# The first four units of a linear-attention and MLP kernel: another order of bonus products, loads, masks and transposes

## The chip, the cores and the metric

The kernel runs on one core of a Trainium2 chip. The metric is the device time of one execution in microseconds (us); several runs are given by their median.

## The reference

The first half is a recurrent attention (RWKV) over batch 4, 8 heads, 768 steps and head size 48. For every head it keeps a 48 x 48 state:

```python
for t in range(S):
    cur = np.einsum('bhd,bhe->bhde', u[None] * kt, vt)
    y[:, :, t] = np.einsum('bhd,bhde->bhe', rt, state + cur)
    state = w[None, :, :, None] * state + np.einsum('bhd,bhe->bhde', kt, vt)
```

The term with u is the bonus of the current step: for each step and head it is the sum over d of r times u times k, times v. The second half takes y as a matrix x of 3072 rows (batch by step) and 384 columns through an MLP: `h = x @ w_in` (384 x 2048), `g = h * sigmoid(h)`, `out = g @ w_out` (2048 x 384).

## The kernel before

The 768 steps are cut into six chunks of 128. A unit is one chunk of one batch entry; unit i is batch i mod 4 of chunk i div 4, so there are 24 units, and units 0 to 3 are the first chunk of the four batch entries. Within a chunk the recurrence is turned into matrix products with decayed r and k.

For unit i the steps have short names, which the order below uses:

- `lr`, `lk`, `lv` (line 71): the loads of r, k and v, 192 KB each, issued on SP's queue. Units 0 to 3 are loaded ahead of the order (lines 103 to 115); k of unit 0 is issued by ScalarE (ACT). Eight buffers of each are there.
- `T` (turn, line 251): 16 transposes on TensorE, eight for r and then eight for k. `rT`, `kT` (line 257): VectorE (DVE) multiplies them with the powers of the decay.
- `A01`, `A23` (line 284): the products of k and r for two units together, 64 small matmuls. `am` (line 291): DVE masks the product, with maskM for even units and maskX for odd ones.
- `ku`, `ru` (lines 211 and 215): the bonus on GpSimd (POOL), k times u and then r times that. `rd` (line 224): DVE sums over d. `vu` (line 229): POOL multiplies v by the sum.
- `v16` (line 238): ACT casts v; for an odd unit two more copies (`vx`, lines 241 and 242) swap its halves.
- `Y` (line 306): masked product times v. `y16` (line 334): DVE adds `vu`. `yT` (line 372): three transposes on TensorE, and `xT` (line 376): ACT copies them to x.
- `kc` (line 219): POOL decays k. `S` (line 318): the state product, and `st` (lines 348 and 349): DVE copies it out.
- `L` and `G` (lines 387 and 395): a block of the first MLP product, with the two units that it covers, and its activation on ACT. `L0.0` and `L0.2` are the first blocks for units 0 and 1, and `L0.4`, `L0.6` need the second quarter of w_in. The second MLP product is at lines 408 and 433.
- `i_q` (line 84) and `i_o` (line 89): loads of a quarter of w_in or w_out, 384 KB, issued by POOL.
- `pads`: ACT fills the unused columns of r and k buffers 4 to 7, eight small copies (line 155). `lnw`, `eK`, `lamK`, `lnwb`, `lamC`, `wb`, `mx`: the powers of the decay, and maskX.
- A prefix `n*` puts n matmuls of 128 x 512 on a tile of zeros (`spin`, line 161) before the step; they compute nothing that is used.

There is no scheduler: the kernel is written under a manual schedule, and an order written out by hand (line 485) is walked from left to right. Each step puts its instructions at the end of its engine's queue, and each engine takes its own in that order, waiting where an operand or a buffer is not ready. So the place of a word in the text counts only against other words of the same engine. Short-lived tiles rotate through buffers (two for most); products, transposed y and MLP blocks share four PSUM buffers.

After this order a loop (line 518) takes the later units in pairs, with pieces of the MLP of the chunk before as filling work for TensorE. The loop calls `bonus_products` (line 205), so the change of the bonus reaches it as well.

Of the kernel before, what the change touches and what calls it, by code (L numbers as in the profile page):

```python
# [8 lines left out]
FP = mybir.dt.float32  # L9
F16 = mybir.dt.float16  # L10
AF = mybir.ActivationFunctionType
ALU = mybir.AluOpType
# [3 lines left out]
def kernel(  # L16
# [11 lines left out]
    nc = tc.nc  # L28

    B, H, S, D = r.shape  # L30
# [10 lines left out]
    NIN = 8  # L41
# [4 lines left out]
    wrk = ctx.enter_context(tc.tile_pool(name="wrk", bufs=2))  # L46
# [3 lines left out]
    def unit(i):  # L50
        return divmod(i, B)
# [9 lines left out]
    u_bc = cst.tile([128, H, D], FP)  # L61
    rin = [big.tile([128, H, 64], FP, name=f"rin{i}") for i in range(NIN)]
    kin = [big.tile([128, H, 64], FP, name=f"kin{i}") for i in range(NIN)]
    vin = [big.tile([128, H, D], FP, name=f"vin{i}") for i in range(NIN)]
    kc = [big.tile([128, H, 64], F16, name=f"kc{i}") for i in range(NIN)]
    st = [big.tile([PR, NP, PW], FP, name=f"st{b}") for b in range(B)]
# [4 lines left out]
    def ld(i, dst, src, eng=nc.sync):  # L71
        sc, b = unit(i)
        eng.dma_start(
            out=dst[i % NIN][:, :, 0:D],
            in_=src[b, :, sc * C:sc * C + C, :].rearrange("h t d -> t h d"))

    def load(i):
        if i >= NU:
            return
        for dst, src in ((rin, r), (kin, k), (vin, v)):  # L80
            ld(i, dst, src)
# [29 lines left out]
                                            ap=[[0, 128], [D, H], [1, D]]))  # L111
    ld(0, vin, v)
    ld(1, vin, v)
    load(2)
    load(3)
    nc.vector.memset(ones, 1.0)
    for i in range(B):
        nc.vector.memset(rin[i][:, :, D:64], 0.0)
# [1 line left out]
    for b in range(B):  # L120
# [13 lines left out]
        out=maskM, in_=maskM, compare_op=ALU.is_ge, fill=0.0,  # L134
# [10 lines left out]
    eK = cst.tile([PR, NP, C], FP)  # L145
    lamR = cst.tile([PR, NP, C], FP)
    lamK = cst.tile([PR, NP, C], FP)
    lnw_bc = cst.tile([128, HD], FP)
    lamC = cst.tile([128, H, D], FP)
# [52 lines left out]
    def L(i):  # L202
        return live.setdefault(i, {})

    def bonus_products(i):
        bonus_ku(i)
        bonus_rku(i)

    def bonus_ku(i):
        L(i)["ku"] = wrk.tile([128, H, D], FP, name="ku")  # L210
        nc.gpsimd.tensor_tensor(out=L(i)["ku"], in0=kin[i % NIN][:, :, 0:D], in1=u_bc, op=ALU.mult)  # L211

    def bonus_rku(i):
        L(i)["rku_f"] = wrk.tile([128, H, D], FP, name="rku_f")
        nc.gpsimd.tensor_tensor(out=L(i)["rku_f"], in0=rin[i % NIN][:, :, 0:D], in1=L(i)["ku"],  # L215
                                op=ALU.mult)

    def decayed_k(i):
        nc.gpsimd.tensor_tensor(out=kc[i % NIN][:, :, 0:D], in0=kin[i % NIN][:, :, 0:D],  # L219
# [246 lines left out]
    def piece(word, f):  # L466
# [11 lines left out]
        "am": masked, "v16": cast_v, "kc": decayed_k,  # L478
        "vu": bonus_v,
        "Y": outputs_y, "S": outputs_s, "y16": evict_y, "yT": turn_y, "xT": copy_x,  # L480
        "st": state, "stb": state16, "ku": bonus_ku, "ru": bonus_rku, "rd": bonus_sum,
        "r16": cast_r, "sd": decayed_state, "i_q": ld_win, "i_o": ld_wout,
        "lr": lambda i: ld(i, rin, r), "lk": lambda i: ld(i, kin, k), "lv": lambda i: ld(i, vin, v),
    }
    order = """
        lnw eK lamK mx clear lr4 lk4 lv4 lr5 lk5 lv5 lr6 lk6 lv6 lr7 lk7 lv7 4*T0 ku0 rT0 kT0
        1*T1 rT1 kT1 v160 ru0 rd0 ku1 v161 3*A01 wb ru1 am0 rd1 vu0 lnwb i_q0 lamC pads am1 vu1
        4*Y0 y160 T2 kT2 2*Y1 y161 ku2 ru2 rT2 yT0 xT0 i_q1 yT1 xT1 v162 T3 kT3 rT3 ku3 ru3 rd2
        v163 4*A23 vu2 i_q2 rd3 vu3 am2 am3 L0.0 G0.0 L0.2 G0.2 Y2 y162 Y3 y163 kc0 yT2 xT2 L0.4
        G0.4 kc1 yT3 xT3 L0.6 G0.6 S0 st0 kc2 T4 kT4 rT4 kc3 L2.0 G2.0 S1 L2.2 G2.2 st1 ku4 v164  # L490
        L2.4 G2.4 S2 L2.6 G2.6 st2 ru4 i_q3 r164 L4.8 G4.8 S3 L4.9 G4.9 st3 rd4 ku5 L4.10 G4.10
        T5 kT5 rT5 L4.11 G4.11 vu4 ru5 i_o0 A45 rd5 am4 r165 v165 L4.12 G4.12 vu5 kc4 L4.13
        G4.13 am5 sd4 kc5 Y4 S4 y164 st4 L4.14 G4.14 sd5 i_o1 Y5 S5 y165 st5 L4.15 G4.15 yT4 xT4
        yT5 xT5 T6 kT6 rT6 ku6 ru6 i_o2 H0 H1 v166 r166 H2 H3 T7 kT7 rT7 ku7 i_o3 v167 r167 H4
        ru7 rd6 stb4 stb5
    """
    for word in order.split():
        if "*" in word:
# [19 lines left out]
    for i in range(B + 2, NU, 2):  # L518
# [3 lines left out]
        if i > B + 2:  # L522
            for n in nxt:
                bonus_products(n)
                decayed_k(n)
        if i > B + 2:
            masked(i)
            masked(i + 1)
        else:
            bonus_v(i)  # L530
            decayed_k(i)
            decayed_state(i)
            masked(i)
            bonus_sum(i + 1)
            masked(i + 1)
            bonus_v(i + 1)
            decayed_k(i + 1)
            decayed_state(i + 1)
            for n in nxt:
                bonus_products(n)  # L540
                decayed_k(n)
# [60 lines left out]
```

## Time and profile before

Durations are in us. "Window" is a stretch of the profiled execution.

| what | value |
| --- | --- |
| median of 13 runs | 195.35 (194.24 to 196.98) |
| the profiled execution: run, and span from first to last instruction | 194.70, 193.0 |
| mean granted TensorE clock of the span | 0.991 |
| one bonus product on POOL, L211 or L215 | 1.00 |
| one `vu` (L229), one `kc` (L219) on POOL | 0.83, 1.00 |
| one sum (L224), one mask (L291), one `y16` (L334), one `rT` or `kT` (L257) on DVE | 0.54, 1.22, 0.56, 0.68 |
| one cast of v (L238), one half of `vx` (L241, L242), one `xT` (L376) on ACT | 0.51, 0.51, 0.48 |
| issue of a quarter of w_in by POOL (L84) | 0.80 to 0.93 |
| a load of r, k or v from issue to landing, median | 4.1 to 4.2 |
| a quarter of w_in from issue to landing, median | 6.8 |
| DMA engines' busy share, 20 to 25 us (overlapping packets count twice) | 1.24 |

One bonus product waited: `ku` of unit 0 for u, 3.2 us. In the first 50 us ACT waited 8.6 us for MLP products, and DVE 3.9 us each for transposes (L251) and for bonus products (L215). From 50 us to 150 us the windows show TensorE busy all the time.

The page gives busy time by engine, then 40 slices of the span with a digit for each engine, then the chain of work that ended last. The timeline gives single instructions with start and length and, in brackets, the idle time before them and what ended it.

### The profile page before, as it was taken

The page shows a single profiled execution, that of the slowest core. Times are in us where ns is not written, and L with a number is a line of the kernel's source. Part 1 is how long each engine was busy: PE and PEld are TensorE (multiplying, and loading weights), DVE is VectorE, ACT ScalarE, POOL GpSimd, SP SyncE. Part 2 cuts the span into 40 slices and gives each one's busy share as a digit, 9 for nine tenths or more (in the row PEclk, how much of TensorE's full clock was granted, in tenths as well). Part 3 has the DMA queues.
Part 4 walks back from the last instruction along what each step waited for, and adds up shares of the span by engine and source line. Part 5 has one row for each costly group of instructions (what it writes and reads, how often), then busy time and mean ns, then how long its engine had stood idle before and what let it go on. Part 6 is the DMA issues. An engine that isn't in the chain of part 4 may idle for free.

```text
span 193.0 us, 5626 instructions
## 1 busy us (share of the span) xinstructions
PE 184.4 (96%) x2306; PEld 118.5 (61%) x2306; DVE 102.7 (53%) x188; ACT 108.3 (56%) x212; POOL 120.2 (62%) x159
## 2 busy tenths in 40 slices
PE   7988899989999999999999999999999999999994
PEld 2644684667766886655556665566655656644563
DVE  6577769764782682672672673673574364200120
ACT  5398277759371493176792276791376781089300
POOL 8399994999999939929829839839837430000000
PEclk9996999999999999999999999999999999999999
DMA  5999979999948568249259278177287101320022
GB/s 103 209 182 158 231 146 179 167 202 220 158 107 176 176 117 193 63 104 199 71 107 200 66 163 187 25 140 170 61 183 168 40 5 44 82 82 0 3 82 82
DMA packets 90267, 24.35 MB, mean 126 GB/s; under 512 B 83329, under 2 KB 90242, under 8 KB 90242
## 3 DMA queue, kind: packets, MB, share of 16 engines
q1 hardware_dynamic: 85136, 20.59, 49.3%
q0 software_dynamic: 3712, 3.15, 10.9%
q10 hardware_dynamic: 1394, 0.26, 0.7%
q8 instruction: 18, 0.29, 0.6%
q14 instruction: 7, 0.06, 0.1%
HBM read 20.65 MB, written 4.72 MB: 131 GB/s over the span
## 4 chain that ended last, share of the span: by engine, by line
PE 76%; POOL 13%; issue 3%; DMA 3%; ACT 2%; SPq 1%; DVE 1%; POOLq 0%
PE ops L408 31%; PE hps L387 27%; PE att L284 7%; PE att L251 4%; POOL ku L211 3%; POOL kc L219 3%; DMA u_bc<-in_u_dram 3%; POOL vu L229 2%; POOL rku_f L215 2%; PE yp L306 2%; PE yp L301 2%; POOL win L84 2%; PE sp L318 1%; PE ops L433 1%; ACT gT L395 1%
## 5 line engine op out<-in xcount | busy, mean ns | idle before, releaser
L387 PE MATMUL hps<-xT,win 128*128 128x512 f16 (+1 forms) x360 | 68.2, 337 | 0.7 <-ACT xT L376 0.5
L395 ACT ACTIVATE gT<-hps 128x512 f16<-128x512 f32 x96 | 56.2, 598 | 21.1 <-PE hps L387 18.9
L408 PE MATMUL ops<-wout,gT 128*128 128x384 f16 x368 | 64.0, 326 | 0.0
L408 PEld LDWEIGHTS <-gT 128*128 128x128 f16 x368 | 34.7, 98 | 22.2
L387 PEld LDWEIGHTS <-win 128*128 128x128 f16 x360 | 33.3, 98 | 24.2 <-issue 1.1
L229 POOL TENSOR_TENSOR vu<-vin,rku 128x384 f32<-128x384 f32 x24 | 19.8, 830 | 27.1 <-DVE rku L224 27.1
L414 ACT COPY osb<-ops 128x384 f32<-128x384 f32 x20 | 9.6, 478 | 43.4 <-PE ops L408 43.4
L291 DVE TENSOR_TENSOR am<-att,maskM 128x1024 f16<-128x1024 f32 x12 | 14.7, 1223 | 32.3 <-PE att L284 32.3
L211 POOL TENSOR_TENSOR ku<-kin,u_bc 128x384 f32<-128x384 f32 x24 | 24.1, 1003 | 4.8 <-DMA u_bc<-in_u_dram 3.2
L215 POOL TENSOR_TENSOR rku_f<-rin,ku 128x384 f32<-128x384 f32 x24 | 24.1, 1002 | 1.7
L219 POOL TENSOR_TENSOR kc<-kin,lamC 128x384 f16<-128x384 f32 x24 | 23.8, 999 | 0.0
L284 PEld LDWEIGHTS att<-rT,kT 48*64 48x64 f32 x768 | 18.0, 135 | 6.7 <-issue 3.5
L284 PE MATMUL att<-rT,kT 48*64 48x128 f32 (+1 forms) x768 | 20.4, 250 | 1.2 <-DVE rT L257 0.8
L257 DVE TENSOR_TENSOR rT<-att,lamR 112x512 f32<-112x512 f32 x24 | 16.4, 684 | 9.3 <-ACT gT L395 4.0
L334 DVE TENSOR_TENSOR y<-yp,vu 128x384 f16<-128x384 f32 x24 | 13.3, 556 | 13.6 <-issue 4.8
L257 DVE TENSOR_TENSOR kT<-att,lamK 112x512 f32<-112x512 f32 x24 | 16.4, 682 | 4.0 <-PE att L251 3.9
L291 DVE TENSOR_TENSOR am<-att,maskX 128x1024 f16<-128x1024 f32 x12 | 14.6, 1214 | 0.0
L224 DVE TENSOR_REDUCE rku<-rku_f 128x8 f32<-128x384 f32 x24 | 12.4, 544 | 3.9 <-POOL rku_f L215 3.9
L329 POOL TENSOR_TENSOR sdec<-st,wCT 112x384 f32<-112x384 f32 x16 | 13.2, 825 | 0.0
L238 ACT CAST v<-vin 128x384 f16<-128x384 f32 x24 | 11.4, 511 | 3.3 <-DMA vin<-in_v_dram 3.3
L272 ACT CAST rT<-rT 112x512 f16<-112x512 f32 x20 | 12.4, 619 | 0.3 <-DVE rT L257 0.2
L306 PEld LDWEIGHTS <-am 128*128 128x128 f16 x192 | 9.7, 97 | 4.3 <-DVE am L291 2.8
(64 smaller groups left out, 161.8 us busy)
## 6 DMA issues: line engine op xcount, KB each, us to landing
rin<-in_r_dram SPq DMA_DIRECT2D x24, 192.0 KB, 4.1
vin<-in_v_dram SPq DMA_DIRECT2D x24, 192.0 KB, 4.2
kin<-in_k_dram SPq DMA_DIRECT2D x23, 192.0 KB, 4.2
out_dram<-osb SPq DMA_DIRECT2D x23, 192.0 KB, 2.2
win<-in_moe_w_in_dram POOLq DMA_DIRECT2D x4, 384.0 KB, 6.8
wout<-in_moe_w_out_dram POOLq DMA_DIRECT2D x4, 384.0 KB, 6.4
xT<-y SPq DMA_TRANSPOSE x18, 2.3
kin<-in_k_dram ACTq DMA_DIRECT2D x1, 192.0 KB, 3.5
```

The lines of the kernel that those rows point to most:

```text
L211: nc.gpsimd.tensor_tensor(out=L(i)["ku"], in0=kin[i % NIN][:, :, 0:D], in1=u_bc, op=ALU.mult)
L215: nc.gpsimd.tensor_tensor(out=L(i)["rku_f"], in0=rin[i % NIN][:, :, 0:D], in1=L(i)["ku"], op=ALU.mult)
L219: nc.gpsimd.tensor_tensor(out=kc[i % NIN][:, :, 0:D], in0=kin[i % NIN][:, :, 0:D], in1=lamC, op=ALU.mult)
L229: nc.gpsimd.tensor_tensor(out=L(i)["vu"], in0=vin[i % NIN], in1=L(i)["rku"].unsqueeze(2).broadcast_to([128, H, D]), op=ALU.mult)
L257: nc.vector.tensor_tensor(out=L(i)[key].rearrange("p g (y t) -> p y g t", y=2), in0=L(i)["t"][0:PR, :, x], in1=lam.rearrange("p g (y t) -> ...
L284: nc.tensor.matmul(a[e][o0:o0 + HC, j, p, c0:C], kT[r0:r0 + D, p, s0:s0 + HC], rT[r0:r0 + D, p, c0:C], start=True, stop=True)
L291: nc.vector.tensor_tensor(out=am.rearrange("p h g c -> p (h g) c"), in0=L(i)["a"].rearrange("p h g c -> p (h g) c"), in1=(maskX if crossed ...
L306: nc.tensor.matmul(L(i)["y"][:, h, :], L(i)["am"][:, j, p, :], L(i)["vy"][:, h, :], start=not sc, stop=(not sc or j == 1))
L334: nc.vector.tensor_tensor(out=L(i)["y16"], in0=L(i)["y"], in1=L(i)["vu"], op=ALU.add)
L387: nc.tensor.matmul(hps[:, f, :], win[:, q, (ft + f) * 128:(ft + f + 1) * 128], xts[sc][:, q, b0:b0 + nb, :].rearrange("p b t -> p (b t)"), ...
L395: nc.scalar.activation(out=gts[sc][:, ft:ft + m, b0 * C:(b0 + nb) * C], in_=hpss[b0, ft], func=AF.Silu)
L408: nc.tensor.matmul(opss[b], gts[sc][:, ft, b * C:(b + 1) * C], wout[:, ft, :], start=(ft == 0), stop=(ft == NFT - 1))
```

## The change

- The bonus is r times k first (`rk`) and the result times u afterwards (`ru`), in all 24 units; before it was k times u and then r times that.
- r and k of units 2 and 3 are issued before v of units 2 and 3. The loads themselves are the same.
- In the order: `rk1` comes before `ru0`; on POOL `vu1` comes before the first weight load, `vu3` and `kc0` before the third; `am0` stands before `ru1` in the text. The transposes `T3` with `kT3` and `rT3` come before `yT1` on TensorE and before `y161` on DVE, and `rT2` comes before `y161`. `yT1` comes behind `A23`, and `xT1` behind the casts of v of units 2 and 3 and behind `pads` on ACT. The eighteen matmuls on zeros are spread otherwise.
- From `yT2` on the order is as before, with `rk` for `ku`.

```diff
-    load(2)
-    load(3)
+    for dst, src in ((rin, r), (kin, k)):
+        ld(2, dst, src)
+    for dst, src in ((rin, r), (kin, k)):
+        ld(3, dst, src)
+    ld(2, vin, v)
+    ld(3, vin, v)
...
     def bonus_products(i):
-        bonus_ku(i)
+        bonus_rk(i)
         bonus_rku(i)
...
-        L(i)["ku"] = wrk.tile([128, H, D], FP, name="ku")
-        nc.gpsimd.tensor_tensor(out=L(i)["ku"], in0=kin[i % NIN][:, :, 0:D], in1=u_bc, op=ALU.mult)
+        L(i)["rk"] = wrk.tile([128, H, D], FP, name="rk")
+        nc.gpsimd.tensor_tensor(out=L(i)["rk"], in0=kin[i % NIN][:, :, 0:D],
+                                in1=rin[i % NIN][:, :, 0:D], op=ALU.mult)
...
-        nc.gpsimd.tensor_tensor(out=L(i)["rku_f"], in0=rin[i % NIN][:, :, 0:D], in1=L(i)["ku"],
-                                op=ALU.mult)
+        nc.gpsimd.tensor_tensor(out=L(i)["rku_f"], in0=L(i)["rk"], in1=u_bc, op=ALU.mult)
...
-        lnw eK lamK mx clear lr4 lk4 lv4 lr5 lk5 lv5 lr6 lk6 lv6 lr7 lk7 lv7 4*T0 ku0 rT0 kT0
-        1*T1 rT1 kT1 v160 ru0 rd0 ku1 v161 3*A01 wb ru1 am0 rd1 vu0 lnwb i_q0 lamC pads am1 vu1
-        4*Y0 y160 T2 kT2 2*Y1 y161 ku2 ru2 rT2 yT0 xT0 i_q1 yT1 xT1 v162 T3 kT3 rT3 ku3 ru3 rd2
-        v163 4*A23 vu2 i_q2 rd3 vu3 am2 am3 L0.0 G0.0 L0.2 G0.2 Y2 y162 Y3 y163 kc0 yT2 xT2 L0.4
+        lnw eK lamK mx clear lr4 lk4 lv4 lr5 lk5 lv5 lr6 lk6 lv6 lr7 lk7 lv7 4*T0 rk0 rT0 kT0
+        1*T1 rT1 kT1 rk1 ru0 rd0 v160 v161 3*A01 wb am0 ru1 vu0 rd1 am1 vu1 lnwb lamC i_q0 1*Y0
+        y160 T2 kT2 rT2 2*Y1 rk2 1*yT0 xT0 ru2 3*T3 kT3 rT3 v162 y161 rk3 i_q1 3*A23 v163 pads
+        yT1 xT1 ru3 rd2 vu2 rd3 vu3 am2 am3 L0.0 G0.0 L0.2 G0.2 Y2 y162 Y3 y163 kc0 i_q2 yT2 xT2
...
```

More of the change, by code (lines that the diff above doesn't have):

```diff
@@ L205, in bonus_products, with bonus_rk @@
     def bonus_products(i):
-        bonus_ku(i)
+        bonus_rk(i)
         bonus_rku(i)
-    def bonus_ku(i):
-        L(i)["ku"] = wrk.tile([128, H, D], FP, name="ku")
-        nc.gpsimd.tensor_tensor(out=L(i)["ku"], in0=kin[i % NIN][:, :, 0:D], in1=u_bc, op=ALU.mult)
+    def bonus_rk(i):
+        L(i)["rk"] = wrk.tile([128, H, D], FP, name="rk")
+        nc.gpsimd.tensor_tensor(out=L(i)["rk"], in0=kin[i % NIN][:, :, 0:D],
+                                in1=rin[i % NIN][:, :, 0:D], op=ALU.mult)
     def bonus_rku(i):
         L(i)["rku_f"] = wrk.tile([128, H, D], FP, name="rku_f")
-        nc.gpsimd.tensor_tensor(out=L(i)["rku_f"], in0=rin[i % NIN][:, :, 0:D], in1=L(i)["ku"],
-                                op=ALU.mult)
+        nc.gpsimd.tensor_tensor(out=L(i)["rku_f"], in0=L(i)["rk"], in1=u_bc, op=ALU.mult)
     def decayed_k(i):
@@ L480 @@
         "Y": outputs_y, "S": outputs_s, "y16": evict_y, "yT": turn_y, "xT": copy_x,
-        "st": state, "stb": state16, "ku": bonus_ku, "ru": bonus_rku, "rd": bonus_sum,
+        "st": state, "stb": state16, "rk": bonus_rk, "ru": bonus_rku, "rd": bonus_sum,
         "r16": cast_r, "sd": decayed_state, "i_q": ld_win, "i_o": ld_wout,
@@ L485 @@
     order = """
-        lnw eK lamK mx clear lr4 lk4 lv4 lr5 lk5 lv5 lr6 lk6 lv6 lr7 lk7 lv7 4*T0 ku0 rT0 kT0
-        1*T1 rT1 kT1 v160 ru0 rd0 ku1 v161 3*A01 wb ru1 am0 rd1 vu0 lnwb i_q0 lamC pads am1 vu1
-        4*Y0 y160 T2 kT2 2*Y1 y161 ku2 ru2 rT2 yT0 xT0 i_q1 yT1 xT1 v162 T3 kT3 rT3 ku3 ru3 rd2
-        v163 4*A23 vu2 i_q2 rd3 vu3 am2 am3 L0.0 G0.0 L0.2 G0.2 Y2 y162 Y3 y163 kc0 yT2 xT2 L0.4
[L490 to L495, printed above, removed]
+        lnw eK lamK mx clear lr4 lk4 lv4 lr5 lk5 lv5 lr6 lk6 lv6 lr7 lk7 lv7 4*T0 rk0 rT0 kT0
+        1*T1 rT1 kT1 rk1 ru0 rd0 v160 v161 3*A01 wb am0 ru1 vu0 rd1 am1 vu1 lnwb lamC i_q0 1*Y0
+        y160 T2 kT2 rT2 2*Y1 rk2 1*yT0 xT0 ru2 3*T3 kT3 rT3 v162 y161 rk3 i_q1 3*A23 v163 pads
+        yT1 xT1 ru3 rd2 vu2 rd3 vu3 am2 am3 L0.0 G0.0 L0.2 G0.2 Y2 y162 Y3 y163 kc0 i_q2 yT2 xT2
+        L0.4 G0.4 kc1 yT3 xT3 L0.6 G0.6 S0 st0 kc2 T4 kT4 rT4 kc3 L2.0 G2.0 S1 L2.2 G2.2 st1 rk4
+        v164 L2.4 G2.4 S2 L2.6 G2.6 st2 ru4 i_q3 r164 L4.8 G4.8 S3 L4.9 G4.9 st3 rd4 rk5 L4.10
+        G4.10 T5 kT5 rT5 L4.11 G4.11 vu4 ru5 i_o0 A45 rd5 am4 r165 v165 L4.12 G4.12 vu5 kc4
+        L4.13 G4.13 am5 sd4 kc5 Y4 S4 y164 st4 L4.14 G4.14 sd5 i_o1 Y5 S5 y165 st5 L4.15 G4.15
+        yT4 xT4 yT5 xT5 T6 kT6 rT6 rk6 ru6 i_o2 H0 H1 v166 r166 H2 H3 T7 kT7 rT7 rk7 i_o3 v167
+        r167 H4 ru7 rd6 stb4 stb5
     """
```

## The prediction

> **What bounds the kernel now.** I read the page first, for who is busy and where the clock fell; then the chain of waits in order of time; then the timeline of the first 27 us engine by engine; last the windows. From the page:
>
> ```profile
> PE 184.4 (96%) x2306; PEld 118.5 (61%) x2306; DVE 102.7 (53%) x188; ACT 108.3 (56%) x212; POOL 120.2 (62%) x159
> ...
> PEclk9996999999999999999999999999999999999999
> ...
> PE 76%; POOL 13%; issue 3%; DMA 3%; ACT 2%; SPq 1%; DVE 1%; POOLq 0%
> ```
>
> TensorE is 96% busy, and one slice, the fourth (14.5 to 19.3 us), had a low clock. The chain, from its list of pieces (start, length, what):
>
> ```profile
> 3.31 4.91 DMA u_bc<-in_u_dram
> ...
> 8.37 1.00 POOL ku L211
> ...
> 22.25 3.86 POOL kc L219 x4
> ...
> 46.07 1.55 PE att L284 x56
> ```
>
> From about 46 us to the end the chain is TensorE alone, so a change of the first units is worth only what it moves that point. Before it the chain names POOL from 8.37 us on. That is a list of who was late, not of how much is gained if POOL is early: the instructions from 15 to 26 us decide that (start, length, engine, line; in brackets the idle time before and its releaser):
>
> ```profile
> 15.56 1.09 ACT L376 COPY xT<-yT 128x384 f16<-128x384 f16 x2
> 16.54 0.93 ACT L238 CAST v<-vin 128x384 f16<-128x384 f32 x2
> 18.02 0.51 ACT L242 COPY vx<-v 64x384 f16<-64x384 f16 x1
> 18.90 1.84 PE L284 MATMUL att<-rT,kT 48*64 48x128 f32 x64
> 20.68 1.48 PE L387 MATMUL hps<-xT,win 128*128 128x256 f16 x12
> 20.80 1.22 DVE L291 TENSOR_TENSOR am<-att,maskM 128x1024 f16<-128x1024 f32 x1 [0.30 <-PE att L284]
> 23.21 0.37 PE L306 MATMUL yp<-vx,am 128*128 128x48 f16 x8 [0.76 <-DVE am L291]
> 25.33 0.33 PE L318 MATMUL sp<-v,kc 128*128 128x96 f16 x4
> 25.70 0.35 DVE L348 CAST stb<-sp 48x192 f16<-48x192 f32 x1 [1.46 <-PE sp L318]
> ```
>
> The point that carries the rest is S0 (the state product of unit 0, L318, 25.33). From 25.70 DVE runs without a gap over 0.04 us until 33.98 (st0, kT4, rT4, st1 to st3, rd4, kT5, rT5); rd4 releases POOL's vu4, which waited 2.4 us, and from there vu4, ru5, vu5, kc4, kc5 and S5 follow to 38.9 and the chain to A67 at 46.07. So I take a shift of S0 as the shift of the end.
>
> ```profile
> 12.71:16.12 3.41, 2.27 (x34) 1.19 (x32) 3.41 (x6) 3.30 (x10) 3.31 (x5) 1.00 0.77 129
> 16.12:19.53 3.41, 3.41 (x33) 1.89 (x36) 1.96 (x4) 2.32 (x5) 3.31 (x4) 0.50 1.10 179
> 19.53:22.94 3.41, 2.92 (x80) 2.44 (x72) 2.69 (x3) 1.19 (x2) 3.39 (x5) 1.00 1.26 226
> ```
>
> These windows (columns: length, then PE, PEld, DVE, ACT, POOL busy, then clock, DMA share, GB/s) are cut at the clock's own edges: after 3.41 us with PE busy 2.27 the clock is 0.50 for 3.41 us; after 2.92 it stays 1.00.
>
> **What the Trainium skill says.** "TensorE: Matmul & The Clock Gate", Part 1, says that the array's clock is halved according to recent activity, judged in free-running windows of 3413 ns. The trace agrees in length (16.12 to 19.53), and in effect: warm-up matmuls (L161) start 0.22 us apart at 7 us and 0.42 at 17 us. The page gives no busy share that decides; the trace brackets it between 2.27 and 2.92. The same page, Part 2, says that matmuls stay in program order and only weight loads are pulled ahead: so L0.0 holds up everything behind it. "DMA: Bandwidth & Descriptors", Queues, rings and completion order, says that each DMA engine takes turns between the queues that have work. The trace fits: v3, issued at 12.71, took 4.2 us to land while the first weight load (issued 13.22) streamed.
>
> **The change part by part**, against this execution (span 193.0, run 194.70; the median of 13 runs is 195.35, 0.65 more).
>
> POOL, r by k first. Same count of products, same shapes, 1.00 us each (rows L211, L215). rk0 needs k0 and r0 (1.42 + 3.5 = 4.9), POOL is free at 5.1: 5.1 to 6.1. rk1 waits for k1 (2.52 + 3.9 = 6.4): 6.6 to 7.6. ru0 still waits for u (3.31 + 4.91 = 8.22): 8.37 to 9.37; ru1 to 10.33. Before they ended at 10.45 and 12.49. So 3.25 us of idle POOL take two products, and the sums come 1.1 and 2.2 us sooner.
>
> Masks. On DVE the order rd0, am0, rd1, am1 stays. rd0 9.40; am0 must wait for A01 (8.56 + 1.55 = 10.11): 10.17 to 11.39; rd1 to 11.87; am1 11.8 to 13.0 (before 14.21). vu1 11.95 to 12.79; first weight load 12.73, 0.5 us sooner. Then rk2 waits for k2, which lands as before (8.21 + 4.8 = 13.0): 13.7 to 14.7, ru2 to 15.75, rk3 to 16.7, second weight load 16.65 (before 17.00), ru3 18.47 (before 19.91). POOL's lead ends at 1.4 us. The third weight load goes behind vu3 and kc0: 20.98 for 20.63. It landed at 28.3 and is used at 29.55: costs nothing with 1.2 us to spare. The fourth comes about 1.4 us sooner, but nothing waits for it there.
>
> Loads. SP issues the same loads with r3 and k3 in the places of v2 and r3. v2 landed at 8.98 + 4.6 = 13.6, k3 at 10.48 + 4.5 = 15.0; so r3 comes at 13.6, k3 by 15.0 at most (I take 14.3), v2 at 15.0. v3 stays last, at 12.71 + 4.2 = 16.9. Bound for the new mix: v3 unchanged, or up to 0.5 us later because the weight load starts 0.5 us sooner and shares the engines. I take 16.9 and keep the other for the range.
>
> TensorE. Eighteen warm-up matmuls before and after, spread otherwise. T2 waits for k2 as before (13.05 to 13.48), two warm-ups, Y1 13.87, one, yT0 14.45, three, T3 at 15.35 instead of 16.06 and at full clock: its window from 12.7 has few holes. T3 ends 16.0 (before 17.15), kT3 and rT3 1.29 us of DVE: 17.35. A23 17.4 to 18.95 at the 1.55 us of A01 (before 18.90 to 20.74). Gain 1.8 us, of which 0.7 from T3's place and the rest from the clock.
>
> Behind it yT1, moved from before T3 to after A23: 18.80 to 19.14. Its copy xT1 is where the gain goes. ACT's order is now xT0, v2, v3, two vx, eight pads, xT1. xT0 14.85 to 15.3, v2 to 15.8, v3 waits for its load: 16.96 as before; vx until 18.53; pads 1.69 us (eight, 0.20 apart): until 20.2; xT1 0.48: about 20.6. L0.0 needs xT1: 20.68, the very time of before. TensorE has nothing from 19.14 to 20.68, and am2 and am3, ready at 20.2 and 21.35 instead of 22.02 and 23.15, wait behind L0.0 and L0.2. What is left: Y2 22.08 as before, Y3 at once (22.35 for 23.21), y2 to 23.06 (before 23.62), yT2 23.12, L0.4 not before the second weight load lands (17.00 + 6.7 = 23.7; I take 23.4), S0 = L0.4 + 1.47 = 24.9. Sum at full clock: 24.92 - 25.33 = -0.4.
>
> But the windows now hold that 1.5 us hole. With the edges of this trace, 19.53 to 22.94 has 1.48 (L0.0, L0.2) plus 0.65 (Y2, Y3), 2.1 busy: less than the 2.27 that halved the clock. Elsewhere in phase, windows from 17.6 to 21.0 or 18.6 to 22.0 have 1.9. Then 3.41 us follow at half clock. With the trace's edges: yT2 0.33, L0.4 0.65 doubled to 1.3, yT3 0.3, L0.6 1.3: S0 at 26.35, +1.0 against before. If it falls on L0.0 and L0.2 (1.30 of issue doubled) and the small steps behind: S0 at 25.9, +0.6. The old low clock is already in the 25.33. I take +0.7.
>
> The steady state: rk reads r and k where ku read k; rows and waits are otherwise the same, buffers of r come free one product sooner (SP's waits for POOL's products there, 2.0 and 1.5 us, end no chain). Zero.
>
> **Rivals.** Forecast: hole and low clock, +0.7, 196.0 (own range 195.7 to 196.6), chance 0.52. For it: the 16.9 of v3 and the ACT order, both free of guesses; against: no trace shows whether 1.9 to 2.1 suffices.
> Rival one, not slower: the clock stays up behind the hole. S0 at 24.9, -0.4: 194.95; it decides if the threshold lies under 1.9 (against: 2.27 halved it), or if the clock falls earlier, in the thin stretch 10.9 to 13.4, where only one warm-up is left before Y0 (about 2.7 busy, between the brackets): then T3 and A23 go slower, the hole closes and the sum is 0 to -0.4. Chance 0.28.
> Rival two: v3 later by 0.5 us with the weight load's start, on top of the low clock: L0.0 21.2, sum +1.2, 196.5. Chance 0.12; against: v3's last packets may be its own.
> Rival three: ACT gets to xT1 sooner than I think (v3 at 16, pads quicker); L0.0 then waits for the first weight load, 20.19 - 0.5 = 19.7, Y2 21.1, Y3 21.4, S0 by the second weight load at 24.6 to 24.9, -0.4 to -0.8: 194.7. Chance 0.08.
>
> **How the numbers follow.** About 0.3% (0.59 us) is what a measurement can tell here. The range goes from 194.8 (rival one and half of three) to 196.8 (rival two and the forecast's worst phase). Slower by over 0.59: two thirds of the forecast, all of rival two and a share for what I have not seen, 0.52. Within: 0.36. Faster: rival three and the edge of rival one, 0.12.
>
> **What would show it.** Right: rk0 near 5.1, ru0 at 8.4, A23 starting near 17.4, xT1 behind the pads near 20.1, TensorE idle before L0.0 at 20.7, a window of clock 0.50 starting between 19.6 and 23.0, S0 later than 25.5. Wrong: L0.0 before 20.3; no low clock after 19 us; S0 before 25; or an end that does not move with S0, which would mean slack after 34 us that I have not seen.

## The result and the profile after

| | before | after |
| --- | --- | --- |
| median | 195.28 of 48 runs (194.24 to 198.23) | 198.59 of 11 runs (196.52 to 200.12) |
| profiled execution: run, span | 194.70, 193.0 | 198.53, 196.8 |
| mean granted TensorE clock of the span | 0.991 | 0.983 |

The changed kernel is slower: its time is 1.0151 of that before, with an interval of 1.0116 to 1.0185, and its median is 3.3 us higher. In this section and the next, ratios leave out executions over 1.5% above the fastest of their own kernel (two of twelve here), which changes the reading of two experiments, where all executions are given too. The lines of the changed kernel stand four higher than before's: L391 is the first MLP product, L380 `xT`, L322 the state product, L242 the cast of v, L245 and L246 `vx`, L159 the pads, L215 `rk`, L220 `ru`.

First the page of after: the engines, the clock in 40 slices, the chain by engine, and the costliest group of TensorE (busy time, mean of one in ns, idle time before it and the releaser). The last line is the same group on the page of before.

```profile
PE 184.8 (94%) x2306; PEld 119.2 (61%) x2306; DVE 102.8 (52%) x188; ACT 108.5 (55%) x212; POOL 120.2 (61%) x159
...
PEclk9999769999999999999999999999999999999999
...
PE 74%; SPq 10%; issue 4%; POOL 4%; DMA 3%; ACT 2%; DVE 1%; POOLq 0%
...
L391 PE MATMUL hps<-xT,win 128*128 128x512 f16 (+1 forms) x360 | 70.1, 344 | 4.0 <-ACT xT L380 3.8
```

```profile
L387 PE MATMUL hps<-xT,win 128*128 128x512 f16 (+1 forms) x360 | 68.2, 337 | 0.7 <-ACT xT L376 0.5
```

No engine has noticeably more work. The row that stands out is L391: in front of it TensorE was idle 0.7 us before and 4.0 us now, nearly all of it for `xT`, and it is busy 70.1 us instead of 68.2 for the same 360 products, which goes with the lower clock (slices five and six, where before had one in slice four). The chain has changed its names as well: POOL went from 13% to 4%, and SP's queue has come up to 10%. Its list of pieces, in order of time (start, length, what), shows where:

```profile
19.06 2.61 SPq L73
21.71 6.42 DMA kin<-in_k_dram
29.28 7.24 issue
...
49.88 1.55 PE att L288 x56
```

The part of A67 at which TensorE takes over starts at 49.88 instead of 46.07: the same 3.8 us as the span. Ahead of it the chain now follows SP and the load of a k. Read as a cause, that would say that the loads of later units are late. Experiment one tests this reading against the other one, which the timeline of the same kernel gives:

```profile
5.32 1.00 POOL L215 TENSOR_TENSOR rk<-kin,rin 128x384 f32<-128x384 f32 x1 [0.20 <-DMA kin<-in_k_dram]
8.38 1.95 POOL L220 TENSOR_TENSOR rku_f<-rk,u_bc 128x384 f32<-128x384 f32 x2 [0.57 <-DMA u_bc<-in_u_dram]
...
17.76 1.55 PE L288 MATMUL att<-rT,kT 48*64 48x128 f32 x60 [0.27 <-DVE rT L261]
...
19.13 0.51 ACT L242 CAST v<-vin 128x384 f16<-128x384 f32 x1 [3.07 <-DMA vin<-in_v_dram]
19.25 0.34 PE L376 MATMUL yT<-ident,y 128*128 128x128 f16 x3
20.20 0.51 ACT L246 COPY vx<-v 64x384 f16<-64x384 f16 x1
20.72 0.30 ACT L159 CAST rin<-idle 128x128 f32<-128x128 f16 x1
22.12 0.29 ACT L159 CAST kin<-idle 128x128 f32<-128x128 f16 x1
22.32 0.47 ACT L380 COPY xT<-yT 128x384 f16<-128x384 f16 x1
22.84 2.72 PE L391 MATMUL hps<-xT,win 128*128 128x256 f16 x12 [3.25 <-ACT xT L380]
29.15 0.33 PE L322 MATMUL sp<-v,kc 128*128 128x96 f16 x4
29.52 0.35 DVE L352 CAST stb<-sp 48x192 f16<-48x192 f32 x1 [2.51 <-PE sp L322]
```

POOL's products, the masks and A23 are as early as they were meant to be. Then ACT waits 3.07 us for v of unit 3, which lands at 19.1; the cast, two `vx` and eight pads follow (20.72 to 22.32 for the pads alone), and only then `xT1`. Its transposes were done at 19.6. L0.0 starts at 22.84 where it started at 20.68, and S0 follows at 29.15 for 25.33. From S0 to TensorE's last instruction it is 164.8 us in both profiles, so the end has moved with S0.

The windows of after show the second half of the loss (length, then PE, PEld, DVE, ACT and POOL busy, clock, DMA share, GB/s):

```profile
18.24:21.65 3.41, 1.35 (x55) 1.16 (x48) 3.18 (x4) 2.46 (x8) 3.25 (x5) 1.00 1.25 220
21.65:25.06 3.41, 2.22 (x11) 1.56 (x11) 0.07 (x1) 1.73 (x6) 3.39 (x5) 0.50 1.09 188
25.06:28.48 3.42, 3.02 (x31) 2.38 (x30) 1.02 (x2) 1.14 (x3) 2.77 (x4) 0.50 1.02 193
```

The hole leaves 1.35 us of work in the first window, and the next one is at half clock. That next one still holds a part of the hole and is busy only 2.22 us; after it the clock stays at 0.50 for one window more. A mean of 0.983 over the span is two such windows; nine of twelve executions of after have that mean to within 0.001, two have 0.991 (one window), one has 0.974.

How late v3 was stands in the DMA issues between 13.2 and 13.8 us (size, then us from issue to landing):

```profile
vin<-in_v_dram SPq DMA_DIRECT2D x1, 192.0 KB, 5.9
...
win<-in_moe_w_in_dram POOLq DMA_DIRECT2D x1, 384.0 KB, 5.7
```

Before, v3 was issued at 12.71 and the first weight load at 13.22, and v3 took 4.2 us. Now the weight load is issued at 12.76 and v3 behind it at 13.18: v3 takes 5.9 us. Whether the one makes the other is asked in experiments three, five and ten.

### The profile page after: what moved, and what is told of

Same layout as the page of the kernel before. It is cut to its first block, busy times and chain, and to the rows that moved or that the text cites. A ratio compares the mean times of both kernels' runs of the same rounds, so it can differ in the third digit from the quotient of the medians.

```text
span 196.8 us, 5624 instructions
## 1 busy us (share of the span) xinstructions
PE 184.8 (94%) x2306; PEld 119.2 (61%) x2306; DVE 102.8 (52%) x188; ACT 108.5 (55%) x212; POOL 120.2 (61%) x159
## 4 chain that ended last, share of the span: by engine, by line
PE 74%; SPq 10%; issue 4%; POOL 4%; DMA 3%; ACT 2%; DVE 1%; POOLq 0%
PE ops L412 31%; PE hps L391 26%; SPq L73 9%; PE att L288 7%; PE att L255 4%; DMA kin<-in_k_dram 3%; PE yp L310 2%; PE yp L305 2%; PE sp L322 1%; PE ops L437 1%; ACT gT L399 1%; POOL kc L223 1%; SPq L110 1%; POOL vu L233 1%; POOL rk L215 1%
## 5 line engine op out<-in xcount | busy, mean ns | idle before, releaser
L391 PE MATMUL hps<-xT,win 128*128 128x512 f16 (+1 forms) x360 | 70.1, 344 | 4.0 <-ACT xT L380 3.8
L391 PEld LDWEIGHTS <-win 128*128 128x128 f16 x360 | 34.1, 100 | 28.3 <-issue 4.5
L233 POOL TENSOR_TENSOR vu<-vin,rku 128x384 f32<-128x384 f32 x24 | 19.8, 829 | 32.8 <-DVE rku L228 32.8
L215 POOL TENSOR_TENSOR rk<-kin,rin 128x384 f32<-128x384 f32 x24 | 24.1, 1005 | 2.5 <-DMA kin<-in_k_dram 2.5
L220 POOL TENSOR_TENSOR rku_f<-rk,u_bc 128x384 f32<-128x384 f32 x24 | 23.9, 999 | 2.1 <-DMA u_bc<-in_u_dram 0.6
L242 ACT CAST v<-vin 128x384 f16<-128x384 f32 x24 | 11.5, 511 | 6.4 <-DMA vin<-in_v_dram 6.4
L333 POOL TENSOR_TENSOR sdec<-st,wCT 112x384 f32<-112x384 f32 x16 | 13.2, 825 | 0.0
L420 DVE COPY osb<-ops 128x384 f32<-128x384 f32 x3 | 1.7, 557 | 19.8 <-PE ops L412 19.8
```

What stands on the lines that cost most here:

```text
L215: nc.gpsimd.tensor_tensor(out=L(i)["rk"], in0=kin[i % NIN][:, :, 0:D], in1=rin[i % NIN][:, :, 0:D], op=ALU.mult)
L220: nc.gpsimd.tensor_tensor(out=L(i)["rku_f"], in0=L(i)["rk"], in1=u_bc, op=ALU.mult)
L233: nc.gpsimd.tensor_tensor(out=L(i)["vu"], in0=vin[i % NIN], in1=L(i)["rku"].unsqueeze(2).broadcast_to([128, H, D]), op=ALU.mult)
L391: nc.tensor.matmul(hps[:, f, :], win[:, q, (ft + f) * 128:(ft + f + 1) * 128], xts[sc][:, q, b0:b0 + nb, :].rearrange("p b t -> p (b t)"), ...
```

## The experiments

The theory was that the loss is the hole in front of L0.0 (`xT1` behind a late v3, `vx` and pads on ACT) and the low clock that it brings; the rival was that the loads are late, as the chain names them. Each kernel is the changed one with the edit shown, unless it says "before with". Ratios are to the kernel before. Only one execution of each kernel is profiled, and the medians are over all its runs; where the two disagree it is said.

**One: pads behind `xT1`.**

```diff
-        ... 3*A23 v163 pads
-        yT1 xT1 ru3 rd2 ...
+        ... 3*A23 v163
+        yT1 xT1 pads ru3 rd2 ...
```

> The changed kernel with the eight pad copies on ACT moved behind xT1; nothing else. Theory (a hole in front of L0.0, made by xT1 behind v3 and the pads, then a low clock): xT1 follows vx at about 20.7 instead of 22.3, L0.0 starts at 21.2 instead of 22.84, and the hole (19.6 to 21.2) still lowers the clock: 1.0 to 2.5 us faster than the changed kernel, so ratio to before 1.003 to 1.010. Rival (the loads: the chain of the changed kernel names SP's queue and the load of k of unit 5): the pads touch no load, so the time stays within 0.5 us of the changed kernel, ratio 1.013 to 1.018.

Measured: 195.99 (12 runs), 1.0012, interval 0.9975 to 1.0049. The timeline:

```profile
20.77 0.48 ACT L380 COPY xT<-yT 128x384 f16<-128x384 f16 x1
...
21.30 1.47 PE L391 MATMUL hps<-xT,win 128*128 128x256 f16 x12 [1.38 <-ACT xT L380]
...
25.34 0.33 PE L322 MATMUL sp<-v,kc 128*128 128x96 f16 x4
```

Its chain, in order of time:

```profile
22.16 6.11 DMA kin<-in_k_dram
...
46.07 1.55 PE att L288 x56
```

v3 landed at 19.1 here too, and no load was moved. Taking 1.6 us of pads from in front of `xT1` gave back 2.6 of the 3.3 us: L0.0 comes 1.54 us sooner, and in this execution the clock never fell, so S0 comes 3.81 us sooner. Of twelve executions two had no low window, eight had one and two had two. The rival falls: the k load that the chain names is the same one, of unit 5, and it lands no sooner here (28.27) than in after (28.14); the chain names it again, and yet TensorE takes over at 46.07, exactly as in before. The gain is a little more than I had expected.

**Two: the hole filled with matmuls on zeros.**

```diff
-        ... am2 am3 L0.0 ...
+        ... am2 am3 12*L0.0 ...
```

> The changed kernel with twelve matmuls on zeros between yT1 and L0.0, 2.6 us that fit into the hole of 3.25 us; nothing else. Theory: L0.0 still starts at 22.8, but the clock stays up, and L0.0 to S0 takes 4.3 us instead of 6.3: 2 us faster than the changed kernel, ratio to before about 1.005 (1.002 to 1.009). Rival (loads): same time as the changed kernel or slower, ratio 1.013 to 1.02. Third reading (the clock is low for another reason than the hole): the clock still falls near 21.7, and the ratio stays at 1.015.

Measured: 197.54 (4 runs), 1.0109, interval 1.005 to 1.0169. The timeline (zs are the added matmuls):

```profile
18.00 2.75 PE L165 MATMUL zs<-idle 128*128 128x512 f16 x12
23.23 1.47 PE L391 MATMUL hps<-xT,win 128*128 128x256 f16 x12 [2.48 <-ACT xT L380]
...
27.28 0.33 PE L322 MATMUL sp<-v,kc 128*128 128x96 f16 x4
```

L0.0 is no sooner (23.23), yet S0 follows after 4.05 us instead of 6.31. So at full clock this stretch takes about 4.05 us (as in experiment one), and with two low windows 2.26 us more. In the medians it gave back only 1.05 us, and the ratio is above the expected 1.002 to 1.009: two of the four executions kept the mean of 0.983, at 198.02 and 198.06, and the two at full clock took 197.01 and 197.06, only 1.0 us less. The wait and the clock are two separate losses; how much the clock costs beyond the profiled stretch is not settled by four executions.

**Three: the old order of the loads.**

```diff
-    for dst, src in ((rin, r), (kin, k)):
-        ld(2, dst, src)
-    for dst, src in ((rin, r), (kin, k)):
-        ld(3, dst, src)
-    ld(2, vin, v)
-    ld(3, vin, v)
+    load(2)
+    load(3)
```

> The changed kernel with the loads of units 2 and 3 in the order of before (r2 k2 v2 r3 k3 v3). Theory in the form of the prediction (v3 is late because the first weight load starts 0.5 us sooner): v3 stays last and still lands at 18.5 to 19.1, time within 0.5 us of the changed kernel, ratio 1.012 to 1.018. Rival (the new order of the loads makes v3 late): v3 lands near 17, L0.0 at 20.7, hole 1.1 us and at most one window of low clock: 2 to 3.5 us faster, ratio 0.997 to 1.005.

Measured: 197.95 (4 runs), 1.0122, interval 1.0057 to 1.0187. v3, issued at 12.72 and the weight load at 12.74, landed at 19.16 all the same, with a hole of 3.75 us and two low windows. So the new order of r, k and v is not needed for a late v3.

**Four and six: `xT1` back in front of T3** (with `y161` and `yT1`), in six with the pads between `v162` and `v163` as well.

```diff
-        y160 T2 kT2 rT2 2*Y1 rk2 1*yT0 xT0 ru2 3*T3 kT3 rT3 v162 y161 rk3 i_q1 3*A23 v163 pads
-        yT1 xT1 ru3 ...
+        y160 T2 kT2 2*Y1 y161 rT2 rk2 1*yT0 xT0 ru2 3*yT1 xT1 T3 kT3 rT3 v162 rk3 i_q1 3*A23 v163 pads
+        ru3 ...
```

> The changed kernel with y161, yT1 and xT1 at their old place, ahead of T3 and of the casts of units 2 and 3, so that L0.0 waits for neither v3 nor pads. Theory: A23 ends at 19.3 as in the changed kernel, L0.0 follows at once at 19.3, Y2 20.8, Y3 21.8, S0 near 24 (25.33 before, 29.15 changed), clock full: 1.0 to 1.5 us faster than before, ratio 0.992 to 0.996. Rival (loads): L0.0 earlier, but S0 or the work behind it waits for loads, ratio 1.005 or more.

> The kernel of run e4 with the eight pad copies between the casts of v2 and v3, where ACT waits 3.1 us for v3 anyway. Theory (in e4 the pads only moved the hole: G0.0 stood behind v3 and the pads, and yT2 waited 1.5 us for a PSUM buffer that G0.0 frees): G0.0 at 20.8 to 21.3, yT2 at 22.1, L0.4 at 22.5 behind the second weight load, S0 at 24.0 instead of 26.0 and of 25.33 before, clock up: ratio 0.991 to 0.996. Rival (loads bind what follows): S0 earlier, but the work from 27 to 38 us waits for k of unit 5 or for the third weight load, ratio 0.998 to 1.002.

Measured: four 195.63 (12 runs), 1.0002, interval 0.9965 to 1.0039; six 195.56 (22 runs), 0.9994, interval 0.9961 to 1.0026. Both expectations missed: the loss is gone, but no gain over before appears. The timeline of four:

```profile
19.15 1.48 PE L391 MATMUL hps<-xT,win 128*128 128x256 f16 x12
...
23.53 0.33 PE L376 MATMUL yT<-ident,y 128*128 128x128 f16 x3 [1.52 <-ACT gT L399]
...
26.02 0.53 PE L322 MATMUL sp<-v,kc 128*128 128x96 f16 x4
```

L0.0 is 1.53 us sooner than before, but ACT then reaches G0.0 only behind v3 and the pads, and the transposes of y2 wait 1.52 us for the PSUM buffer that G0.0 frees. In six, with the pads out of the way, the next wait is there:

```profile
23.21 1.46 PE L391 MATMUL hps<-xT,win 128*128 128x256 f16 x6 [1.01 <-DMA win<-in_moe_w_in_dram]
```

L0.4 waits for the second quarter of w_in. Of the 20 executions behind the ratio of six, eight ran at full clock (0.998 or higher): six of them took 193.59 to 194.03, two 195.25 and 195.47. Ten had one low window and two had two; the median of these twelve is 195.92. So the clock goes with most of that difference, but not with all of it.

**Five: the first weight load behind `rk2`.**

```diff
-        ... lamC i_q0 1*Y0
-        y160 T2 kT2 rT2 2*Y1 rk2 1*yT0 ...
+        ... lamC 1*Y0
+        y160 T2 kT2 rT2 2*Y1 rk2 i_q0 1*yT0 ...
```

> The changed kernel with the first weight load on POOL moved behind rk2, about 2 us later (issue near 14.8 instead of 12.76); nothing else. Theory (the weight load, started sooner, takes the DMA engines from v3, the last of the eager loads): v3 lands near 17 instead of 19.1, xT1 at 20.2, L0.0 at 20.8 (both the copy and the weight load ready there): 1.5 to 3 us faster than the changed kernel, ratio to before 1.000 to 1.008. Rival (v3 is late for another reason, such as how its own issue falls): v3 still lands after 18.5, ratio 1.012 to 1.018.

Measured: 195.91 (20 runs), 1.0023, interval 1.0002 to 1.0045. First the DMA issue of v3 (13.8 to 14.4 us), then the timeline:

```profile
vin<-in_v_dram SPq DMA_DIRECT2D x1, 192.0 KB, 3.5
```

```profile
21.82 2.00 PE L391 MATMUL hps<-xT,win 128*128 128x256 f16 x12 [1.82 <-DMA win<-in_moe_w_in_dram]
```

v3 is issued later than in after (13.78 for 13.18) and lands 1.86 us sooner (17.25), with the weight load now behind it (15.04). That is what was expected of the weight load's place ahead of v3, and the ratio lies in the expected range; the landing itself is known from one execution. L0.0 then waits for the weight load instead, with one low window behind it, so that the time only comes level.

**Seven and eleven: before with the change of the bonus alone** (`rk` for `ku` everywhere, `rk1` ahead of `ru0`); eleven also puts the first weight load behind `vu1`.

```diff
-        1*T1 rT1 kT1 v160 ru0 rd0 ku1 v161 3*A01 wb ru1 am0 rd1 vu0 lnwb i_q0 lamC pads am1 vu1
+        1*T1 rT1 kT1 v160 rk1 ru0 rd0 v161 3*A01 wb ru1 am0 rd1 vu0 lnwb i_q0 lamC pads am1 vu1
```

> The kernel before with the bonus part alone: r by k first in all units, rk1 ahead of ru0; loads, masks and transposes as before. Theory: ru0 ends at 9.4 and ru1 at 10.3 as in the changed kernel, the first weight load is issued near 11.3 (13.22 before) and v3 lands later than 17, but xT1 stands ahead of v3 here, so L0.0 does not wait for it: between 0.8 us faster and 0.5 us slower than before, ratio 0.996 to 1.003. Rival (the bonus products themselves cost, by waiting for r and k together): ratio 1.005 or more.

> Run e7 (the kernel before with the bonus part alone) with the first weight load on POOL behind vu1, so that it is issued near 12.8 instead of 11.3. Theory (in e7 the products were quicker as meant, but the weight load that follows them came 1.9 us sooner and put off k of unit 3 from 15.0 to 17.3, so that TensorE waited 1.4 us for it): k3 lands by 15.5, T3 starts by 16, A23 by 18, ratio to before 0.996 to 1.002, below the 1.006 of e7. Rival (the bonus products cost by themselves, by waiting for r and k): ratio as in e7, 1.003 to 1.008.

Measured: seven 196.68 (20 runs), 1.0058, interval 1.0034 to 1.0083: the new bonus alone makes the kernel slower, against what was expected, though its products take 1.0 us each as before and come sooner. The timeline of seven, with POOL's issue of the weight load and the transposes of k3:

```profile
11.30 0.93 POOL L84 DMA_DIRECT2D win<-in_moe_w_in_dram  x1
...
17.30 0.44 PE L251 MATMUL att<-ident,kin 64*112 64x64 f32 x8 [1.38 <-DMA kin<-in_k_dram]
```

POOL is done sooner, so the weight load is issued at 11.30 instead of 13.22; k3 lands at 17.26 instead of 15.0, and TensorE waits for it in T3. This profile itself shows a span of 192.9 at full clock, but 18 of 20 executions have one to three low windows, and the loss is in those (196.1 to 197.8; the two at full clock took 194.64 and 195.26). That the wait in T3 brings those windows is argued. Eleven issues the weight load at 12.83: k3 lands at 15.16 and T3 runs without that wait:

```profile
15.24 0.40 PE L251 MATMUL att<-ident,kin 64*112 64x64 f32 x8
...
19.32 1.49 PE L387 MATMUL hps<-xT,win 128*128 128x256 f16 x12 [0.74 <-DMA win<-in_moe_w_in_dram]
```

Its ratio is 0.9965, interval 0.9931 to 0.9999, but that leaves out eight of its 22 executions; the median of all is 195.69, against 195.10 for before in the same sitting. I do not call it a gain. What it shows, by one profile each, is that the wait in T3 goes when the weight load is held back.

**Eight, nine and twelve: what would beat before?** Eight is six with matmuls on zeros in the waits (`4*T2`, `1*Y2`, `3*Y3`, `4*L0.4`); nine is before with `3*yT1` and `3*Y3`; twelve is six with the second weight load straight behind the first, `am2` ahead of `rd3`, and `v163` behind G0.2 (the diff is twelve's).

```diff
-        ... lamC i_q0 1*Y0
+        ... lamC i_q0 i_q1 1*Y0
...
-        ru3 rd2 vu2 rd3 vu3 am2 am3 L0.0 G0.0 L0.2 G0.2 Y2 ...
+        ru3 rd2 vu2 am2 rd3 vu3 am3 L0.0 G0.0 L0.2 G0.2 v163 Y2 ...
```

> The kernel of run e6 with twelve more matmuls on zeros in waits that its profile shows: four ahead of T2 (wait for k2), one ahead of Y2, three ahead of Y3 (waits for the masks), four ahead of L0.4 (wait of 1.0 us for the second weight load). Theory (in e6 the eleven runs or so near 193.6 to 194.3 have the clock up, those from 195.3 have one low window): most runs keep the clock up and take 193.6 to 194.3, ratio to before 0.991 to 0.996. Rival (the low window is not set by these waits): still two groups of runs, ratio 0.997 to 1.002. Third: the added matmuls take PSUM buffers and delay, ratio above 1.0.

> The kernel before with six more matmuls on zeros: three ahead of yT1 (wait of 0.72 us for y1) and three ahead of Y3 (wait of 0.76 us for the mask); nothing of the change. Theory: the low window of before (16.12 to 19.53 in its profile) goes in most runs, which is worth what it cost there, some 0.4 us: ratio 0.996 to 0.999. Rival (a low clock there costs nothing, L0.0 then waits for its weight load): ratio 0.999 to 1.001.

> The kernel of run e6 with the second weight load straight behind the first on POOL, the sum of unit 3 behind the mask of unit 2 on DVE, and the cast and swap of v3 behind G0.2 on ACT. Theory (L0.4 in e6 waited 1.0 us for the second weight load, and nothing here needs v3 before Y3): second weight load at 20.5 to 22, L0.4 at 22.5, S0 at 24.0 against 25.33 before, ratio 0.990 to 0.997. Rival (two weight loads in a row put off k3 or v3 so far that T3 or Y3 waits): ratio 1.000 or more.

Measured: eight 195.90 (9 runs), 1.0053, interval 1.0029 to 1.0077; nine 195.59 (20 runs), 1.0027, interval 1.0004 to 1.005; twelve 195.82 (22 runs), 1.0029, interval 1.0004 to 1.0054. The theories had all three faster; none was. Eight and nine kept the clock full (0.998 or higher) in every execution, and were still not faster: before's own executions at full clock in the same sitting have a median of 194.58, so nine loses 1.0 us by something else. Its profile shows a part of that. S0 comes at 25.04, 0.29 us sooner than before, and so does A67 (45.08 for 45.38), but then TensorE waits for a quarter of w_out, which it does not do in before's profile:

```profile
52.92 1.46 PE L408 MATMUL ops<-wout,gT 128*128 128x384 f16 x8 [0.47 <-DMA wout<-in_moe_w_out_dram]
```

The profiled span is 193.3. In eight L0.4 waits for its weights:

```profile
25.41 0.83 PE L391 MATMUL hps<-xT,win 128*128 128x256 f16 x6 [1.03 <-DMA win<-in_moe_w_in_dram]
```

In twelve the second weight load is issued at 13.86 instead of 16.66 (six) and lands at 23.41 instead of 23.17: issued sooner it was not there sooner. Now v3 lands at 19.57, and its copies are late for Y3:

```profile
23.09 0.36 PE L310 MATMUL yp<-vx,am 128*128 128x48 f16 x8 [1.95 <-ACT vx L246]
```

**Ten: before with the order of ACT alone** (`yT1 xT1` behind A23, pads between `v163` and `xT1`; bonus and loads as before).

```diff
-        ... lamC pads am1 vu1
+        ... lamC am1 vu1
...
-        ... xT0 i_q1 yT1 xT1 v162 T3 ...
-        v163 4*A23 vu2 ...
+        ... xT0 i_q1 v162 T3 ...
+        v163 pads 4*A23 yT1 xT1 vu2 ...
```

> The kernel before with one part of the change alone: yT1 and xT1 behind A23, and the pads behind the casts of v3 and ahead of xT1 on ACT; bonus, loads, masks and weight loads as before. Theory (the part that the prediction reckoned, with v3 at 17): xT1 at 20.2, L0.0 at 20.7 to 21.0, a hole of about 1.2 us in front of it, one low window behind it in most runs: 0.3 to 1.3 us slower than before, ratio 1.002 to 1.007. Rival (the order alone makes the whole loss): ratio 1.012 or more.

Measured: a median of 197.19 over 16 executions (194.39 to 199.03). The ratio of 1.0025 (0.9992 to 1.0057) holds only the eight faster ones; the other eight are at 197.7 to 199.0. The profiled execution is one of those. In the same sitting one of before's 42 executions took over 197.0. The timeline of ten:

```profile
19.83 0.51 ACT L238 CAST v<-vin 128x384 f16<-128x384 f32 x1 [3.84 <-DMA vin<-in_v_dram]
...
23.02 0.47 ACT L376 COPY xT<-yT 128x384 f16<-128x384 f16 x1
...
23.54 2.72 PE L387 MATMUL hps<-xT,win 128*128 128x256 f16 x12 [4.13 <-ACT xT L376]
```

v3 was issued at 13.27, level with the weight load (13.22), and landed at 19.8; S0 came at 28.89 and the span is 196.5. So the order on ACT makes the whole loss by itself in this execution, where v3 was late with the bonus and the loads of before. In the other half of the executions the loss was small (a median of 195.46, against 194.99 for before); that v3 came in time there is argued, since none of them is profiled. The ratio lies where the theory put it, and the slower half where the rival did.

## Why the prediction was wrong

By its own steps:

- **S0 carries the end: right.** S0 moved by 3.82 us and the span by 3.8. From S0 to the first matmul of A67 it is 20.04 us in before, after, one, nine and ten alike (20.2 to 20.4 in four, six and eleven).
- **POOL, masks, T3, A23: right, a little early.** rk0 at 5.32 (said: 5.1), the first ru at 8.38 (8.37), am1 at 11.83 (11.8), T3 at 15.71 (15.35, as k2 landed at 13.5 and not 13.0), the last 60 of A23's 64 matmuls at 17.76 (17.4). The gain up to A23 is real, and the end sees nothing of it.
- **The place of the hole: right.** `xT1` behind v3, `vx` and pads on ACT, TensorE idle in front of L0.0; experiment one shows it.
- **The landing of v3: here the prediction failed.** It took 16.9, "unchanged, or up to 0.5 us later because the weight load starts 0.5 us sooner". It landed at 19.1: issued 0.47 us later and 1.7 us longer on the way (5.9 us for 4.2). So L0.0 came at 22.84 and not at 20.68: +2.16 us where the sum had nothing. The 16.9 was one execution's landing of a load that nothing waited for, as `xT1` stood ahead of it on ACT. In the profiles of nine and ten, which leave the loads, the bonus and POOL's order as they were in before, v3 landed at 20.38 and 19.81: a late v3 needs no change of any of the three, and 16.9 was one draw from a spread that a single profile of before cannot show. The change made v3 the carrier of L0.0, and then the spread of that landing counted. Rival two named a part of the mechanism but sized it by the shift of the weight load's start. Over the fourteen profiles, one of each kernel, the order of issue goes with the time that v3 took: issued behind the weight load or less than 0.3 us ahead of it, v3 took 5.0 to 6.9 us (ten kernels, after among them), and 3.5 to 4.2 at least 0.5 us ahead of it (before, five, eight; six, 1.1 us ahead and with 7.1, is the exception). The Trainium skill, "DMA: Bandwidth & Descriptors", Queues, rings and completion order, says that an engine takes turns between the queues with work; the prediction used this for a load that shares with a later one, and did not ask what the turns do to a load that comes second. The turns themselves are in no profile here, only the landings.
- **The low clock: right in kind, too small.** The sum had L0.0 to S0 at 4.24 us at full clock and about 1.1 for one window of low clock. Measured: 4.05 at full clock, and 2.26 for the clock, as two windows were low. (The 4.24 had L0.4 wait for the second weight load until 23.4, with 6.7 us added to the issue of before, 17.00, and not to its own 16.65; it landed at 21.7, and L0.4 did not wait for it.) The hole was 3.25 us instead of 1.5, and reached into the window that should have raised the clock again. The phase of the windows has a part in it too: in ten a hole of 4.13 us brought one low window.
- **What halves the clock: not known.** The prediction read a bracket from before: 2.27 us of work in 3.41 lowers the clock, 2.92 keeps it. The profile of after breaks it. Cut back from its own clock edges in steps of 3.41 us, it has a window with less work and a longer gap, behind which the clock stays full:

```profile
11.41:14.83 3.42, 1.99 (x36) 1.47 (x37) 2.88 (x6) 2.48 (x4) 2.74 (x4) 1.00 0.77 148
14.83:18.24 3.41, 3.14 (x46) 1.75 (x48) 2.33 (x5) 0.89 (x2) 3.39 (x4) 1.00 1.18 184
```

This window holds most of the thin stretch of rival one, which put it at about 2.7. The forecast's own doubt, whether 1.9 to 2.1 busy is little enough to lower the clock, was in place.

- **The sum.** Said: 0 for L0.0, -0.4 for the stretch behind it, +1.1 for the clock: +0.7. Measured in the profile: +2.16, -0.60 and +2.26: +3.82.
- **Pads: priced, but not read as a choice.** The 1.69 us were in the sum (1.60 measured), as a step between two other waits. With v3 late they stood wholly on the path, and together with the clock behind them they cost more than themselves (experiment one: 2.6 us in the medians).

Open: what in a window decides whether the clock stays, and why the number of low windows differs from execution to execution; what sets v3's landing, as with 18.68 in six, although it was issued 1.1 us ahead of the weight load; and the rest of what nine loses behind A67.

## What to carry to other kernels

Before moving a copy behind another on the same in-order engine, ask what the one ahead waits for: a load with slack becomes the carrier of everything behind it, and its landing must then be priced with its spread and not with the one landing that the profile shows. An engine made faster issues its own DMAs sooner, and these can put off loads that somebody waits for; hold such an issue where it was, or check who waits. Where the chain of waits names a queue in the changed profile, move the suspected instruction first: here a word moved on ACT gave back 2.6 of 3.3 us without touching the loads that the chain named.

## What was not expected of the hardware

- No share of busy time parts the windows that lower the clock from those that do not. Cut in steps of 3.41 us from each profile's own clock edges, the clock fell from full to half behind windows with at most 1.61 us of work out of 3.41 in seven profiles (1.35 in after, 1.61 in four) and behind one with 2.27 in before; it did not fall behind windows with 1.84 (five), 1.99 (after), 2.22 (four) and 2.34 (three). One long gap does not part them either: the longest in before's window was 0.72 us, and in that of after with 1.99 it was 1.32. To raise the clock again, 2.73 us of work in the window was enough (ten), and 2.22 was not (after).
- The Trainium skill, "TensorE: Matmul & The Clock Gate", Part 1, says that the windows run freely and that what a kernel sees of them varies from run to run; the executions agree: of 167 executions of before, in four sittings, 84 ran at full clock (median 194.86), 75 had one low window (195.55) and 8 had two. A low window went with 0.7 us there.
- Keeping the clock full did not pay by itself: in nine all 20 executions ran at full clock, at 1.0027 of before, and in eight all nine, at 1.0053.
- A weight quarter issued 2.8 us sooner landed 0.24 us later (twelve against six, one profile each).
